# Converting the weights of a feed-forward early: bit work on float64 weights during attention, a float32 copy in DRAM, and a first chunk that only splits

## The chip, the cores and the metric

The kernel runs on one core of a Trainium2 chip. The time is that of the device in microseconds for one execution; of several runs the median counts. TensorE (PE) multiplies matrices, DVE (VectorE), ACT (ScalarE) and POOL (GpSimd) work on elements, SP (SyncE) issues the DMAs.

## The reference

```python
scores = scale * q @ k.T - log(S)            # 8 batches, 12 heads, S = 448, head_dim 64
x = heads_side_by_side(sigmoid(scores) @ v)  # (8, 448, 768)
u = x + real(fft(fft(x, axis=1), axis=2))    # mixing
un = (u - mean(u)) / sqrt(var(u) + 1e-6)     # over the last axis
out = u + maximum(un @ w_ch1, 0) @ w_ch2     # 768 -> 3072 -> 768
```

q, k and v are float32. The two weight matrices are float64.

## The kernel before

**Attention and mixing.** Two heads make a group g; 48 groups (G), six for a batch. A group has four steps t (192 in all): `scores(t)` makes the scores of 112 keys for two heads in PSUM (`sc`, two buffers), ACT makes the sigmoid `a` (L126, five buffers), and two steps later `values(t)` multiplies by v into the one bank `av`. After the fourth step DVE copies `av` into `xT` (L151). Because the f32 matmuls are rounded, q and k are split in two parts: POOL rounds (`cast`, L107: `qh`, `kh`), DVE subtracts (`rest`, L112: `ql`, `kl`). A batch's Fourier transform is done by matrices (`mix_units`): POOL and a little DVE fold xT (`fold`, L165 to L171), TensorE multiplies (`psd`, `pss`) and transposes (`psx`), DVE adds `u` (L223), SP stores `u` in DRAM (`u_dram`). These units are spread over the steps of the next batch.

**Order.** The code is written out in pairs of steps: first what the pair before left over (`flush`: sp_next, act_next, dve_next), then scores, values, mixing units, and then whatever a table `extra` has for these steps; `at(t, fn)` puts something there. `pin` keeps each engine's instructions in the order in which the code names them, so an engine that waits for one instruction holds all behind it. All DMAs go through SP's queue.

**Weights.** A matrix has 24 slices (NFC) of 128 x 768 float64, so 48 slices of 768 KB. Each is read twice. First, during attention: `weight_load` brings it into one of three buffers `wr` (pairs of int32), and `weight_max` on DVE takes the largest absolute high word (L254). At step TP = 170 `weight_scales` makes one scale per matrix. Then, from step TP on, `prep_w` reads each slice again (L356) and converts it: ACT takes the absolute high word (L365, n = 1), DVE clamps and shifts (L367, L369, n = 2), DVE joins low word and sign (L373, L375, n = 3), and in n = 4 ACT scales (L381) and rounds to float16 (`w1h` or `w2h`, L382) and POOL subtracts (`w1l` or `w2l`, L383). The result of n = 1 to 4 stands in one of three buffers `wt`. `prep_step` spreads these parts over slots, two for each f of the first chunk.

**Feed-forward.** There are 7 chunks c of 512 tokens. `norm` normalises a chunk: it loads `un` from `u_dram`, DVE takes statistics and an inverse root in many small operations on `mv` (L297 to L319), DVE scales (L322), ACT rounds to float16 in a buffer `hl` that has the tag `wt` too (L328), DVE subtracts (L332), SP transposes into `uh`, `ul` (L334). For each f of 24, `up_proj` is 18 matmuls into `psh` (L516), ACT and DVE make `hh` and `hl` (L523, L524), and `down_proj` of the f before is 24 matmuls into `po` (L535). `finish` adds `u` and stores. Between attention and the first chunk the rest of the mixing runs (`mix_rest`), with slots in between.

Of the kernel before, what the change touches and what calls it, by code (L numbers as in the profile page):

```python
# [36 lines left out]
LNT = 2  # L37
UNIT_US = 0.57
MIX_UP = 8
MIX_STEP = 7  # L40
# [10 lines left out]
def spectral_attention_ffn(tc, q, k, v, w1, w2, cd, cs, ident_in, out):  # L51
# [8 lines left out]
    with ExitStack() as top:  # L60
        cpool = top.enter_context(tc.tile_pool(name="cpool", bufs=1))
        dram = top.enter_context(tc.tile_pool(name="dram", bufs=1, space=DRAM))
        u_dram = dram.tile([NT, DM], F32, name="u_dram")
        ident = cpool.tile([128, 128], F32, name="ident")
# [13 lines left out]
        if True:  # L78
# [178 lines left out]

            def weight_scales():
# [4 lines left out]

                wi = ws.bitcast(I32)
                nc.vector.tensor_scalar(
                    out=wi[:, 0:2], in0=wi[:, 0:2], scalar1=20, scalar2=0x7FF,
                    op0=ALU.logical_shift_right, op1=ALU.bitwise_and)
                nc.vector.tensor_scalar(
                    out=wi[:, 0:2], in0=wi[:, 0:2], scalar1=1023 - 60, scalar2=1023 + 60, op0=ALU.max, op1=ALU.min)
                nc.vector.tensor_scalar(  # L270
                    out=wi[:, 0:2], in0=wi[:, 0:2], scalar1=-896, scalar2=1 << 23, op0=ALU.add, op1=ALU.mult)
# [80 lines left out]
            def prep_w(i, f, n):  # L352

                if n == 0:
                    prep[i, f] = r = wpre.tile([128, DM, 2], I32, tag="wr", name="wr", bufs=3)
                    nc.sync.dma_start(  # L356
                        r.rearrange("p n w -> p (n w)"), (w1, w2)[i][:, f * 2 * DM:(f + 1) * 2 * DM])
                    return
                if n == 1:
                    prep[i, f] = prep[i, f], wpre.tile([128, DM], F32, tag="wt", name="wt", bufs=3)  # L360
                r, t = prep[i, f]
                ti = t.bitcast(I32)
                lo, hi = r[:, :, 0], r[:, :, 1]
                if n == 1:
                    nc.scalar.activation(t, hi.bitcast(F32), AF.Abs)  # L365
                elif n == 2:
                    nc.vector.tensor_scalar(  # L367
                        out=t, in0=t, scalar1=HI_MIN, scalar2=HI_MAX, op0=ALU.max, op1=ALU.min)
                    nc.vector.tensor_scalar(  # L369
                        out=ti, in0=ti, scalar1=3, scalar2=0x3FFFFFF8,  # L370
                        op0=ALU.logical_shift_left, op1=ALU.bitwise_and)
                elif n == 3:
                    nc.vector.scalar_tensor_tensor(  # L373
                        out=ti, in0=lo, scalar=29, in1=ti, op0=ALU.logical_shift_right, op1=ALU.bitwise_or)
                    nc.vector.scalar_tensor_tensor(  # L375
                        out=ti, in0=hi, scalar=-0x40000000, in1=ti, op0=ALU.bitwise_and, op1=ALU.bitwise_or)
                elif n == 4:
                    h, l = (x[f] for x in ((w1h, w1l), (w2h, w2l))[i])
                    if i == 0:
# [303 lines left out]
```

## Time and profile before

| what | value |
|---|---|
| median of 3 runs | 1817.26 us (1816.38 to 1821.08) |
| profiled execution | 1819.07 us, its span 1817.3 us |
| TensorE busy | 1748.8 us (96%) |
| DVE busy | 677.1 us (37%) |
| ACT busy | 434.2 us (24%) |
| POOL busy | 278.5 us (15%) |
| DMA | 166.56 MB, mean 92 GB/s |
| granted clock of TensorE, mean | 0.992 |

The span goes from the first to the last instruction. The shares are means over stages that differ: attention runs to about 447 us, the rest of the mixing to 470, the first chunk to 690, and six more chunks follow. A granted clock of 1.00 is 2.4 GHz, the upper of two levels; the lower is 1.2 GHz.

### The profile page before, as it was taken

The numbers are of one execution on the slowest core, as the hardware profiler recorded it, in microseconds if no ns is written. First come the engines' busy times: TensorE is split into PE (matmuls) and PEld (weight loads), VectorE is DVE, ScalarE is ACT, GpSimd is POOL, SyncE is SP. The second block draws the span as 40 slices with busy tenths as digits, with TensorE's granted clock in tenths as the row PEclk, the third lists the DMA queues.
The fourth block names the chain that finished last, engine by engine and source line by source line (L and its number), as shares of the span: only waits on it lengthen the run. The fifth ranks groups of instructions, "written<-read, shape, count | busy, mean of one in ns | idle before, by whom it ended". The sixth has DMA issues, their size and how long they took to land.

```text
span 1817.3 us, 22712 instructions
## 1 busy us (share of the span) xinstructions
PE 1748.8 (96%) x9616; PEld 927.0 (51%) x9616; DVE 677.1 (37%) x1143; ACT 434.2 (24%) x581; POOL 278.5 (15%) x268
## 2 busy tenths in 40 slices
PE   8999999988888889999999999999999999999998
PEld 4555555545444445555555555555555555555554
DVE  3445576656999985200320033002400200010001
ACT  4434444435556641000100001000100000000000
POOL 4534444335344430000000000000000000000000
PEclk9999999999999999999999999999999999999999
DMA  7666677654555535000400040004000400010000
GB/s 233 217 210 207 234 222 223 206 188 118 173 170 174 170 127 152 4 1 1 136 4 1 1 122 18 1 1 122 18 1 1 105 18 1 1 43 11 1 1 35
DMA packets 92280, 166.56 MB, mean 92 GB/s; under 512 B 49697, under 2 KB 62738, under 8 KB 92050
## 3 DMA queue, kind: packets, MB, share of 16 engines
q1 hardware_dynamic: 92178, 165.11, 29.3%
q8 instruction: 75, 1.23, 0.3%
q14 instruction: 27, 0.22, 0.0%
HBM read 132.05 MB, written 22.02 MB: 85 GB/s over the span
## 4 chain that ended last, share of the span: by engine, by line
PE 59%; DVE 13%; DMA 2%; issue 1%; ACT 0%; DVEq 0%; ACTq 0%; SPq 0%
PE po L535 30%; PE psh L516 30%; DVE wt L375 5%; DVE wt L373 2%; DVE wt L369 1%; DVE wt L367 1%; DMA un<-u_dram 1%; DVE hl L524 1%; DMA y_out<-ur 1%; DVE ur L556 0%; DVE stt L297 0%; DVE hl L332 0%; DVE u L223 0%; DVE un L322 0%; DVE mv L317 0%
## 5 line engine op out<-in xcount | busy, mean ns | idle before, releaser
L535 PE MATMUL po<-w2h,hl 128*128 128x512 f16 (+1 forms) x1344 | 439.9, 327 | 26.8 <-DVE hl L524 26.8
L535 PE MATMUL po<-w2h,hh 128*128 128x512 f16 (+1 forms) x1344 | 439.9, 327 | 5.0 <-ACT hh L523 4.3
L535 PE MATMUL po<-w2l,hh 128*128 128x512 f16 (+1 forms) x1344 | 439.6, 327 | 0.0
L524 DVE SCALAR_TENSOR_TENSOR hl<-psh,hh 128x512 f16<-128x512 f32 x168 | 115.6, 688 | 833.1 <-ACT hh L523 833.1
L516 PE MATMUL psh<-uh,w1h 128*128 128x512 f16 x1008 | 382.0, 379 | 0.0
L516 PE MATMUL psh<-ul,w1h 128*128 128x512 f16 x1008 | 382.0, 379 | 0.0
L516 PE MATMUL psh<-uh,w1l 128*128 128x512 f16 x1008 | 382.0, 379 | 0.0
L535 PEld LDWEIGHTS <-hh 128*128 128x128 f16 x2688 | 262.5, 98 | 182.6 <-ACT hh L523 12.7
L523 ACT ACTIVATE hh<-psh 128x512 f16<-128x512 f32 x168 | 99.8, 594 | 942.1 <-PE psh L516 942.1
L516 PEld LDWEIGHTS <-w1h 128*128 128x128 f16 x2016 | 197.3, 98 | 236.7
L126 ACT ACTIVATE a<-sc 112x900 f32<-112x900 f32 x192 | 166.7, 918 | 161.1 <-PE sc L122 161.1
L535 PEld LDWEIGHTS <-hl 128*128 128x128 f16 x1344 | 131.9, 98 | 123.1 <-DVE hl L524 38.1
L142 PE MATMUL av<-a,vr 112*64 112x450 f32 x768 | 169.6, 563 | 3.5 <-DVE xT L151 3.5
L516 PEld LDWEIGHTS <-w1l 128*128 128x128 f16 x1008 | 98.6, 98 | 118.9
L375 DVE SCALAR_TENSOR_TENSOR wt<-wr,wt 128x768 int32<-128x768 int32 x48 | 100.4, 2092 | 1.7
L122 PE MATMUL sc<-qh,kh 64*112 64x450 f32 x384 | 81.7, 421 | 10.8 <-ACT a L126 5.2
L142 PEld LDWEIGHTS av<-a,vr 112*64 112x64 f32 x768 | 47.4, 138 | 82.0 <-issue 67.3
L151 DVE TENSOR_SCALAR xT<-av 128x450 f32<-128x450 f32 x48 | 30.1, 626 | 135.0 <-PE av L142 134.9
L184 PEld LDWEIGHTS psd<-cd_sb,xp 128*113 128x113 f32 x384 | 61.1, 178 | 32.8 <-issue 29.7
L184 PE MATMUL psd<-cd_sb,xp 128*113 128x193 f32 x384 | 74.7, 338 | 1.8 <-DVE xp L171 1.8
L122 PE MATMUL sc<-qh,kl 64*112 64x450 f32 x384 | 73.6, 379 | 1.7 <-DVE kl L112 1.7
L122 PE MATMUL sc<-ql,kh 64*112 64x450 f32 x384 | 73.3, 377 | 0.0
(61 smaller groups left out, 1115.8 us busy)
## 6 DMA issues: line engine op xcount, KB each, us to landing
wr<-w_in SPq DMA_DIRECT2D x96, 768.0 KB, 4.7
qr<-q_in SPq DMA_DIRECT2D x48, 225.0 KB, 3.5
kr<-k_in SPq DMA_DIRECT2D x48, 224.0 KB, 3.1
vr<-v_in SPq DMA_DIRECT2D x24, 448.0 KB, 4.0
un<-u_dram SPq DMA_DIRECT2D x14, 768.0 KB, 5.6
ur<-u_dram SPq DMA_DIRECT2D x14, 768.0 KB, 5.6
y_out<-ur SPq DMA_DIRECT2D x12, 768.0 KB, 7.4
u_dram<-u SPq DMA_DIRECT2D x24, 336.0 KB, 3.8
```

The costliest lines, as they stand in the source:

```text
L122: nc.tensor.matmul(ps[:CP, j, :SQ], split[g, 1, kn][h, c * CP:(c + 1) * CP], split[g, 0, qn][h], start=(n == 0), stop=(n == 2))
L126: nc.scalar.activation(a, ps[:CP, :, :SQ], AF.Sigmoid, bias=-math.log(S), scale=1.0 / math.sqrt(D))
L142: nc.tensor.matmul(ps[j * D:(j + 1) * D, :SQ], vr[:, c, h * D:(h + 1) * D], a[:, j], start=(c == 0), stop=(c == 3))
L151: nc.vector.tensor_scalar(out=xT[:, p].rearrange("d r k -> d (r k)"), in0=ps[:, :SQ], scalar1=1.0, scalar2=None, op0=ALU.mult)
L184: nc.tensor.matmul(ps[:HM, par * 193:par * 193 + 193], xp[:, kp ^ c, c, par, p], cd_sb[:, c, par, p], start=(p == 0), stop=(p == 2))
L367: nc.vector.tensor_scalar(out=t, in0=t, scalar1=HI_MIN, scalar2=HI_MAX, op0=ALU.max, op1=ALU.min)
L373: nc.vector.scalar_tensor_tensor(out=ti, in0=lo, scalar=29, in1=ti, op0=ALU.logical_shift_right, op1=ALU.bitwise_or)
L375: nc.vector.scalar_tensor_tensor(out=ti, in0=hi, scalar=-0x40000000, in1=ti, op0=ALU.bitwise_and, op1=ALU.bitwise_or)
L516: nc.tensor.matmul(hs[c, f], l[f][:, m], r[:, m], start=(m == n == 0), stop=(m == NCC - 1 and n == 2))
L523: nc.scalar.activation(hh, ps, AF.Relu)
L524: nc.vector.scalar_tensor_tensor(out=hl, in0=ps, scalar=0.0, in1=hh, op0=ALU.max, op1=ALU.subtract)
L535: nc.tensor.matmul(po[n][:, at:at + hi - lo], l[:, cols], r[f][:, lo:hi], start=(f == 0 and m == 0 and at == 0), stop=(f == NFC - 1 and m ...
```

## The change

During attention each slice is now loaded once and converted there (`weight_step`): load (k = 0, five steps ahead), absolute value on ACT (k = 1), clamp on POOL (k = 2), shift and low word on DVE (k = 3), sign and maximum on DVE (k = 4), and a store of the float32 slice into a DRAM tensor `w_dram` (k = 5). The first chunk's slots load 384 KB of float32, two slots ahead (`AHEAD`); ACT scales and rounds in one operation, DVE makes the low part. Chunk 1's norm moves from attention into chunk 0. The first slots after attention come every four instead of seven steps of the mixing rest.

```diff
+AHEAD = 2
-MIX_STEP = 7
+MIX_STEP = 4
...
+        w_dram = dram.tile([2 * NFC, 128, DM], F32, name="w_dram")
...
-            def weight_max(n):
-                i, f = divmod(n, NFC)
-                nc.vector.tensor_reduce(
-                    out=wmax[:, i, f:f + 1], in_=wtile.pop(n)[:, :, 1].bitcast(F32), op=ALU.max, axis=AX.X,
-                    apply_absolute_value=True)
+            def weight_step(n, k):
+
+                i, f = divmod(n, NFC)
+                if k == 0:
+                    wtile[n] = r = wpre.tile([128, DM, 2], I32, tag="wr", name="wr", bufs=3)
+                    nc.sync.dma_start(
+                        r.rearrange("p n w -> p (n w)"), (w1, w2)[i][:, f * 2 * DM:(f + 1) * 2 * DM])
+                    return
+                if k == 1:
+                    wtile[n] = wtile[n], wpre.tile([128, DM], F32, tag="wt", name="wt", bufs=3)
+                r, t = wtile[n]
+                ti = t.bitcast(I32)
+                lo, hi = r[:, :, 0], r[:, :, 1]
+                if k == 1:
+                    nc.scalar.activation(t, hi.bitcast(F32), AF.Abs)
+                elif k == 2:
+                    nc.gpsimd.tensor_scalar(
+                        out=t, in0=t, scalar1=HI_MIN, scalar2=HI_MAX, op0=ALU.max, op1=ALU.min)
+                elif k == 3:
+                    nc.vector.tensor_scalar(
+                        out=ti, in0=ti, scalar1=3, scalar2=0x3FFFFFF8,
+                        op0=ALU.logical_shift_left, op1=ALU.bitwise_and)
+                    nc.vector.scalar_tensor_tensor(
+                        out=ti, in0=lo, scalar=29, in1=ti, op0=ALU.logical_shift_right, op1=ALU.bitwise_or)
+                elif k == 4:
+                    nc.vector.scalar_tensor_tensor(
+                        out=ti, in0=hi, scalar=-0x40000000, in1=ti, op0=ALU.bitwise_and, op1=ALU.bitwise_or)
+                    nc.vector.tensor_reduce(
+                        out=wmax[:, i, f:f + 1], in_=t, op=ALU.max, axis=AX.X, apply_absolute_value=True)
+                else:
+                    nc.sync.dma_start(w_dram[i * NFC + f], t)
+                    del wtile[n]
...
+            def prep_step(k):
+
+                if k < len(order):
+                    prep[k] = t = wpre.tile([128, DM], F32, tag="wt", name="wt", bufs=3)
+                    i, f = order[k]
+                    nc.sync.dma_start(t, w_dram[i * NFC + f])
+                k -= AHEAD
+                if k in prep:
...
+                    sc = wsc[:, i:i + 1]
+                    nc.scalar.activation(h, t, AF.Copy, scale=sc)
+                    nc.vector.scalar_tensor_tensor(
+                        out=l, in0=t, scalar=sc, in1=h, op0=ALU.mult, op1=ALU.subtract)
...
+            for n in range(2 * NFC):
+                t = 14 + n * (TP - 20) // (2 * NFC)
+                for j, d in enumerate((-5, 0, 1, 2, 3, 5)):
+                    at(t + d, lambda n=n, j=j: weight_step(n, j))
             at(TP, weight_scales)
...
+            for j in range(NPRE + AHEAD):
+                at(TP + (2 if j < AHEAD else 4 * (j - AHEAD) + 6), lambda j=j: prep_step(j))
+            for g in range(2):
+                for n, fn in norm_plan(0, g, fx):
+                    at(24 * (4 + g) + LNT + n, fn)
...
-                n = step % MIX_STEP
-                if n < 4 and slot < NPRE + 2 * NW2:
-                    prep_step(slot, n)
-                    slot += n == 3
+                if step % MIX_STEP == 0 and slot < NPRE + 2 * NW2:
+                    prep_step(slot + AHEAD)
+                    slot += 1
...
-                    if 2 <= c + 1 < NCK:
+                    if c + 1 < NCK:
```

Left out of the diff: the removal of `weight_load`, `prep_w` and the old `prep_step`, and `weight_scales`, which now takes the power of two of the scale by one mask instead of shift and multiply.

DVE's order in attention, in a group of four steps of a batch whose mixing is at its `u` additions. Before (one `xT` to the next):

```order
L151 TENSOR_SCALAR xT<-av 128x450
L254 TENSOR_REDUCE wmax<-wr 128x1
L112 TENSOR_TENSOR ql<-qr,qh 128x450
L112 TENSOR_TENSOR kl<-kr,kh 128x448
L204 TENSOR_TENSOR sm<-pss,Q 112x385
L204 TENSOR_TENSOR df<-pss,Q 112x385
L223 TENSOR_TENSOR u<-psx,df 113x384
L223 TENSOR_TENSOR u<-psx,sm 113x384 x2
L151 TENSOR_SCALAR xT<-av 128x450
```

The same group after the change, with one slice's operations (L266 to L274):

```order
L153 TENSOR_SCALAR xT<-av 128x450
L114 TENSOR_TENSOR ql<-qr,qh 128x450
L114 TENSOR_TENSOR kl<-kr,kh 128x448
L266 TENSOR_SCALAR wt<-wt 128x768
L269 SCALAR_TENSOR_TENSOR wt<-wr,wt 128x768
L206 TENSOR_TENSOR sm<-pss,Q 112x385
L206 TENSOR_TENSOR df<-pss,Q 112x385
L272 SCALAR_TENSOR_TENSOR wt<-wr,wt 128x768
L274 TENSOR_REDUCE wmax<-wt 128x1
L225 TENSOR_TENSOR u<-psx,df 113x384
L225 TENSOR_TENSOR u<-psx,sm 113x384 x2
L153 TENSOR_SCALAR xT<-av 128x450
```

One maximum has become a shift, two joins and a maximum, ahead of the additions `u` and the next `xT`.

SP's order after the change where the first half of chunk 0's norm ends, with buffer numbers: wt_2479 is a slice, hl_2538 and hl_2582 are the norm's, and hl_2582 is the third buffer of the tag `wt` after wt_2479 (between them hl_2538 and wt_2570), so it takes that slice's place.

```order
L252 DMA wr_2533<-w2_in 128x1536
L353 DMA_TRANSPOSE uh_2536<-hl_2538 128x6x128
L353 DMA_TRANSPOSE ul_2537<-hl_2538 128x6x128
L98 DMA kr_2577<-k_in 128x448
L99 DMA qr_2576<-q_in 128x450
L277 DMA w_dram_61<-wt_2479 128x768
L252 DMA wr_2621<-w2_in 128x1536
L353 DMA_TRANSPOSE uh_2536<-hl_2582 128x6x128
```

The store that frees wt_2479 stands behind two transposes and two loads; before there were no stores of slices and no `wt` tiles in these steps. ACT's order at the same place:

```order
L128 ACTIVATE a_2557<-sc_2550 112x900
L261 ACTIVATE wt_2570<-wr_2431 128x768
L347 ACTIVATE hl_2582<-un_2277 128x768
L128 ACTIVATE a_2591<-sc_2584 112x900
L128 ACTIVATE a_2600<-sc_2593 112x900
```

Two sigmoids stand behind hl_2582; before, the absolute value was not there.

DVE's order in the first chunk, from one `hl` to the next, before:

```order
L524 SCALAR_TENSOR_TENSOR hl<-psh,hh 128x512
L367 TENSOR_SCALAR wt<-wt 128x768
L369 TENSOR_SCALAR wt<-wt 128x768
L373 SCALAR_TENSOR_TENSOR wt<-wr,wt 128x768
L375 SCALAR_TENSOR_TENSOR wt<-wr,wt 128x768
L367 TENSOR_SCALAR wt<-wt 128x768
L369 TENSOR_SCALAR wt<-wt 128x768
L373 SCALAR_TENSOR_TENSOR wt<-wr,wt 128x768
L375 SCALAR_TENSOR_TENSOR wt<-wr,wt 128x768
L524 SCALAR_TENSOR_TENSOR hl<-psh,hh 128x512
```

After:

```order
L511 SCALAR_TENSOR_TENSOR hl<-psh,hh 128x512
L386 SCALAR_TENSOR_TENSOR w2l_4733<-wt,wsc,w2h_4712 128x768
L386 SCALAR_TENSOR_TENSOR w1l_4694<-wt,wsc,w1h_4687 128x768
L511 SCALAR_TENSOR_TENSOR hl<-psh,hh 128x512
L386 SCALAR_TENSOR_TENSOR w2l_4734<-wt,wsc,w2h_4713 128x768
L386 SCALAR_TENSOR_TENSOR w1l_4695<-wt,wsc,w1h_4688 128x768
L511 SCALAR_TENSOR_TENSOR hl<-psh,hh 128x512
```

Eight operations between two `hl` have become two.

## Rows read from the trace of the kernel before

**Rows 1.** Windows by stage: TensorE, weight loads, DVE, ACT, POOL busy; clock, DMA share, GB/s.

```profile
0.00:100.00 100.00, 93.25 (x565) 47.93 (x566) 45.41 (x61) 47.88 (x57) 46.04 (x59) 1.00 0.71 222
100.00:200.00 100.00, 95.16 (x578) 53.47 (x578) 46.48 (x70) 43.06 (x55) 41.52 (x49) 0.98 0.63 207
200.00:300.00 100.00, 94.78 (x574) 52.34 (x571) 70.25 (x130) 43.10 (x55) 40.68 (x48) 0.98 0.68 222
300.00:400.00 100.00, 90.71 (x536) 49.82 (x535) 58.91 (x109) 43.37 (x55) 38.40 (x44) 0.97 0.68 216
470.00:690.00 220.00, 190.28 (x969) 93.05 (x969) 205.64 (x239) 122.03 (x152) 82.51 (x43) 0.98 0.51 163
690.00:1818.00 1128.00, 1121.07 (x6053) 591.86 (x6051) 198.56 (x444) 99.60 (x162) 0.00 (x0) 1.00 0.11 31
```

**Rows 2.** Waits of TensorE: who for whom, us, times, longest.

```profile
PE po L535 <- DVE hl L524: 26.8, 22, 3.1
PE psx L216 <- DVE u L223: 13.8, 7, 2.7
```

**Rows 3.** Timeline of DVE, two starts of hl in the first chunk.

```profile
492.55 0.68 DVE L524 SCALAR_TENSOR_TENSOR hl<-psh,hh 128x512 f16<-128x512 f32 x1
501.90 0.68 DVE L524 SCALAR_TENSOR_TENSOR hl<-psh,hh 128x512 f16<-128x512 f32 x1
```

**Rows 4.** Timeline of TensorE at 470 us, then the chain of waits near the end.

```profile
470.07 0.38 PE L535 MATMUL po<-w2h,hh 128*128 128x512 f16 x1 [0.72 <-DVE u L223]
...
1781.38 3.90 PE po L535 x24
1785.28 3.88 PE psh L516 x18
1804.73 5.00 PE po L535 x30
```

**Rows 5.** Groups of instructions by form, whole execution.

```profile
L375 DVE SCALAR_TENSOR_TENSOR wt<-wr,wt 128x768 int32<-128x768 int32 x48 | 100.4, 2092 | 1.7
L254 DVE TENSOR_REDUCE wmax<-wr 128x1 f32<-128x768 f32 x48 | 45.3, 944 | 0.0
L365 ACT ACTIVATE wt<-wr 128x768 f32<-128x768 f32 x48 | 43.4, 904 | 0.7 <-DMA wr<-w_in 0.7
L107 POOL TENSOR_SCALAR kh<-kr 128x448 fp32r<-128x448 f32 x48 | 30.4, 632 | 6.1 <-DMA kr<-k_in 6.1
L369 DVE TENSOR_SCALAR wt<-wt 128x768 int32<-128x768 int32 x48 | 27.4, 570 | 1.6
L332 DVE TENSOR_TENSOR hl<-un,hl 128x768 f16<-128x768 f32 x28 | 26.3, 956 | 20.6 <-ACT hl L328 20.5
```

**Rows 6.** Timeline of DVE, then of POOL.

```profile
420.20 0.96 DVE L375 SCALAR_TENSOR_TENSOR wt<-wr,wt 128x768 int32<-128x768 int32 x1
480.93 2.28 DVE L375 SCALAR_TENSOR_TENSOR wt<-wr,wt 128x768 int32<-128x768 int32 x1
...
480.76 1.64 POOL L383 TENSOR_TENSOR w2l<-wt,w2h 128x768 f16<-128x768 f32 x1 [2.74 <-ACT w2h L382]
```

**Rows 7.** Instructions of tile wr: count, ns min/median/max, first and last start.

```profile
L254 DVE TENSOR_REDUCE wmax<-wr x48: 898/944/992, 33.2 to 372.1; 128x1 f32<-128x768 f32 x48
```

**Rows 8.** Groups of DVE from 100 to 200 us, then its timeline.

```profile
L112 DVE TENSOR_TENSOR kl<-kr,kh 128x448 fp32r<-128x448 f32 x11 | 9.9, 898 | 0.0
L112 DVE TENSOR_TENSOR ql<-qr,qh 128x450 fp32r<-128x450 f32 x11 | 8.2, 745 | 0.0
L151 DVE TENSOR_SCALAR xT<-av 128x450 f32<-128x450 f32 x10 | 6.3, 627 | 42.7 <-PE av L142 42.7
...
122.58 0.61 DVE L112 TENSOR_TENSOR kl<-kr,kh 128x448 fp32r<-128x448 f32 x1
```

**Rows 9.** Timeline of ACT and TensorE at 422 us.

```profile
421.78 0.84 ACT L328 ACTIVATE hl<-un 128x768 f16<-128x768 f32 x1 [7.12 <-DVE un L322]
423.97 0.72 PE L122 MATMUL sc<-qh,kh 64*112 64x450 f32 x2 [4.58 <-ACT a L126]
```

More of the change, by code (lines that the diff above doesn't have):

```diff
@@ L262, in weight_scales @@
                 nc.gpsimd.partition_all_reduce(ws[:, 0:2], wm, 128, bass_isa.ReduceOp.absmax)
+                nc.vector.tensor_scalar(
+                    out=ws[:, 0:2], in0=ws[:, 0:2], scalar1=2.0 ** -60, scalar2=2.0 ** 60, op0=ALU.max, op1=ALU.min)
                 wi = ws.bitcast(I32)
                 nc.vector.tensor_scalar(
[L266 to L271, printed above, removed]
+                    out=wi[:, 0:2], in0=wi[:, 0:2], scalar1=0x7F800000, scalar2=None, op0=ALU.bitwise_and)
                 nc.vector.reciprocal(ws[:, 2:4], ws[:, 0:2])
@@ L350, in spectral_attention_ffn @@
                 order += [(1, f)] + [(0, f + NPRE)] * (f + NPRE < NFC)
[L352 to L377, printed above, removed]
+            def prep_step(k):
[5 more added lines that the diff above has]
+                if k in prep:
+                    i, f = order[k]
+                    t = prep.pop(k)
                     h, l = (x[f] for x in ((w1h, w1l), (w2h, w2l))[i])
@@ L380, in prep_w @@
                         h, l = (x.rearrange("p c f -> p (c f)") for x in (h, l))
-                    nc.scalar.activation(t, t, AF.Copy, scale=wsc[:, i:i + 1])
-                    nc.scalar.activation(h, t, AF.Copy)
-                    nc.gpsimd.tensor_tensor(out=l, in0=t, in1=h, op=ALU.subtract)
-            def prep_step(k, n):
-                for d, m in (((2, 0), (-1, 4)), ((1, 1),), ((0, 2),), ((0, 3),))[n]:
-                    if k + d < len(order) and (k + d, m) not in prepped:
-                        prepped.add((k + d, m))
-                        prep_w(*order[k + d], m)
+                    sc = wsc[:, i:i + 1]
+                    nc.scalar.activation(h, t, AF.Copy, scale=sc)
+                    nc.vector.scalar_tensor_tensor(
+                        out=l, in0=t, scalar=sc, in1=h, op0=ALU.mult, op1=ALU.subtract)
             act_next, dve_next, sp_next, units = [], [], [], []
@@ L437, in spectral_attention_ffn @@
             TP = max(TQ - 4 * NPRE - 10, 1)
-            when_w = {}
-            for n in range(2 * NFC):
-                when_w.setdefault(14 + n * (TP - 14) // (2 * NFC), []).append(n)
             extra = {}
@@ L489, in spectral_attention_ffn @@
                         fn()
-                    for n in when_w.get(i - 1, ()):
-                        weight_load(n + 2)
-                    for n in when_w.get(i, ()):
-                        weight_max(n)
                 pin()
@@ L598, in spectral_attention_ffn @@
                     for n in range(2):
-                        if c == 0 and slot <= len(order):
-                            for step in range(4):
-                                prep_step(slot, step)
+                        if c == 0 and slot < len(order):
+                            prep_step(slot + AHEAD)
                             slot += 1
```

17 lines of the change are left out of this document (removed).

## The prediction

> **What bounds the kernel now.** The windows come first [rows 1]. From 690 us to its last matmul's end at 1809.73 TensorE is never idle (1121.07 us busy by modelled ends), so nothing there can gain. Between 470 and 690 us, the feed-forward's first chunk, TensorE is busy 190.28 of 220 us and DVE 205.64: DVE is the full engine there. Before 400 us TensorE is 91 to 95% busy, DVE 45 to 70%, POOL 38 to 46%. The waits of TensorE say the same [rows 2]: the longest sum is for `hl`, which stands in DVE's queue behind two weight slices. The timeline gives that loop's period [rows 3]: `hl` starts at 492.55 and at 501.90, so 9.35 us for one f. Later chunks show what TensorE alone needs [rows 4]: 3.90 us for a down projection and 3.88 for an up projection, 7.783 us for the pair (three pairs from 1781.38 to 1804.73).
>
> **What the first chunk gives back.** The first down projection starts at 470.07 and the last ends at 1804.73 + 5.00 = 1809.73 [rows 4]: 1339.66 us. At TensorE's own pace it would be 166 pairs x 7.783 + 2 x 3.90 = 1299.8 us (two up projections are done before). The 39.9 us between them are DVE's: 22 f x 1.57 = 34.5 us, the rest the start of the chunk and a clock that fell after waits.
> After the change a slice costs DVE one scalar_tensor_tensor over 768 elements, f32 in and f16 out. The nearest row is the f16 `hl` of the norm at 956 ns [rows 5]; two of them and one 0.68 us `hl` are 2.6 us of the 7.8 us that TensorE needs, where a slice's four operations filled (9.35 - 0.68) / 2 = 4.3 us. ACT loses the absolute value and one of two copies for each slice, POOL its whole part, and the DMA reads half the bytes. Chunk 1's norm moves into this chunk, as it runs in every later one, where TensorE never waits. I keep 1.5 us for the start: **-38 us**. Bounds: 30 (if a wait at the start and the extra norm stay) to 40.
>
> **What attention pays on DVE.** Before, a slice cost DVE one maximum, 944 ns. It keeps that (over contiguous data now) and gets a shift-and (570 ns), and two scalar_tensor_tensor, each 957 ns when nothing is in the way [rows 5, 6]: 0.57 + 2 x 0.957 = 2.48 us more. The 48 maxima ran from 33.2 to 372.1 us [rows 7], 7.1 us apart or 339 / 150 = 2.26 us a step, and the new plan has nearly the same pace, so 14 slices in 100 us: +35 us of DVE in 100.
> On top come waits for POOL. The row to see [rows 6]: the same scalar_tensor_tensor took 0.96 us at 420.20 and 2.28 us at 480.93, where it began while POOL's subtraction (480.76, 1.64 us) ran, and ended 0.8 us after it. That it waits out POOL's instruction is what the Trainium skill says in "SBUF — State Buffer", Who interferes with whom: a DVE operation with two SBUF inputs and a GpSimd operation that reads SBUF exclude each other for a whole instruction. By that rule each new operation with two inputs is exposed, where the free 0.96 us alone would make the sum some 19 us better. How much of it counts is read from attention itself, where `kl` and `ql` average 898 and 745 ns [rows 8] against 610 when free (122.58 in [rows 8]), so 0.2 us an operation with POOL 42% busy. The clamp goes to POOL; there is no such operation of 768 elements in the trace; its bounds are the cast of 448 elements, 0.63 us [rows 5], and the subtraction, 1.64 us; I take the cast by length, 768/448 x 0.632 = 1.08. 14 clamps make POOL 57% busy, so I price the wait at 0.27 us: 3 x 14 x 0.27 = 11 us, and 2 for `ql` and `kl`, in 100. Bounds of the wait: 0 and 1.3 us an operation.
> So DVE's load in 100 us [rows 1]: 100 to 200, 46.5 + 35 + 13 = **94**; 200 to 300, where chunk 0's norm stands, 70.3 + 48 = **118**; 300 to 400, less about 10 for half of chunk 1's norm (the two halves of chunk 0's are most of the 24 us by which 200 to 300 exceeds 100 to 200) and with slices up to 372, 58.9 - 10 + 0.72 x 48 = **83**; 0 to 100, 45.4 + 0.67 x 48 = **78**. DVE was idle 42.7 us in 100 to 200 waiting for `av` alone [rows 8]: that idle time is the cover, and it is used up.
>
> **What that does to TensorE.** `xT` empties the only `av` bank and stands in DVE's queue; TensorE needs it one step later, and `psx` waits for `u` already in each batch (13.8 us in all, [rows 2]). In the order of the change, the four steps with the first `u` get 2.5 us more of DVE; the next four get two shift-ands and three scalar_tensor_tensor for one maximum, 3.2 us more, some 10.0 in all with each operation at 0.5 to 1 us. Nine of these are exposed, 2.4 us: 12.4 us against the 4 x 2.26 = 9.0 of the steps and the 2 that TensorE waits for `u` there already. About +2 us in each of the four to five batches that have slices and no norm: **+10**, and **+6** for uneven steps and clock. In 200 to 320 us the overload of 18 in 100 us ends on TensorE: **+18**. A second wait falls in the same place: `hl` of the norm and the weight tiles share three buffers `wt`; the second `hl` on ACT takes the buffer of a slice whose store is queued on SP behind two transposes, and the sigmoids stand behind that `hl`. The trace has one such case [rows 9]: ACT idle 7.12 us before `hl`, TensorE 4.58 us (such stalls also cost clock: 0.97 and 0.98 are granted here, [rows 1]). Twice that and its clock, some 12 us, lies within the 18, since DVE catches up meanwhile. That very stall, from chunk 1's norm, goes away: **-5**. Attention: 10 + 6 + 18 - 5 = **+29**; bounds 10 (no waits for POOL: DVE 82 and 105 in 100) and 55 (0.5 us an operation).
>
> Free, with what covers it: ACT's 48 absolute values (904 ns, [rows 5]) against an ACT 43% busy; stores of 48 x 384 KB, 14 x 0.393 MB in 100 us or 55 GB/s more on DMA engines 0.63 to 0.71 busy at 207 to 222 GB/s [rows 1], about 0.87; if that cover went, a late `wr` would hold ACT's queue and with it the sigmoids. SP gets 48 stores that wait for DVE; behind them stand `kr`, `qr` loads with five steps (11 us) to spare. The scales lose one operation on two elements.
>
> **Sum.** 1817.3 - 38 + 29 = 1808; of the waits in the mixing rest (0.72 us stands before the first down projection, [rows 4]) 1 us goes too: **1807 us** of span. The profiled execution took 1819.07 us, 1.8 above the median of 1817.26, so on the median's scale the change is -10: 1807.
>
> **Rivals.**
> 1. Attention hides more: the waits for POOL seldom meet, or DVE's lateness is bridged by the five `a` buffers. For it: TensorE's largest wait there, for `u`, is 13.8 us in eight batches. Against it: 118 in 100 cannot be hidden. Attention +12: 1790 us.
> 2. Slower, by DVE and POOL excluding each other. In a batch (24 steps, 55 us) POOL now works 0.415 x 55 = 23 us and then 7.7 x 1.08 = 8 more, and the exposed DVE work is 12 x 0.61 + 7.7 x 2.48 = 26 us: together more than the batch itself. If the two queues alternate, as in the first chunk, where the mean of 2092 ns says that some 41 of 48 took the long time, each operation waits 0.5 to 0.6 us and DVE is over 100 in 100 throughout. It decides from a mean wait of about 0.4 us. Five batches x 5, norm 25, clock 8, less 5: +53; 1832 us. The Trainium skill's rule (the section above) speaks for this rival.
> 3. No change within 0.3% (5.5 us, about what a measurement here can tell): attention takes back 33 to 44 us, the same mechanism at 0.33 us an operation: 1817 us.
> 4. The first chunk is held by something else: `w_dram` loads late behind transposes on SP. Against it: a slice is used four f, 31 us, after its slot. 1820 us.
>
> **Chances.** Forecast (1799 to 1812) 0.38; rival 1 (1782 to 1799) 0.24; rival 3 0.16; rival 2 0.18; rival 4 0.04. Faster: 0.38 + 0.24 less a little for the forecast's upper edge, 0.60; within 0.3%: 0.18; slower: rival 2 and half of 4, 0.22. Range: from rival 1's price, 1788, to rival 2's, 1832; the likeliest's own is 1799 to 1812.
>
> **What would show it.** First chunk: `hl` 7.8 us apart, TensorE over 98% busy, DVE under 50%. Attention: DVE over 90% busy in 100 to 300 us, scalar_tensor_tensor means of 1.2 us, TensorE's idle time ended by `u`, `xT` and ACT, its clock under 1.00, and the mixing rest beginning 25 to 35 us later than before. It is wrong if scalar_tensor_tensor in attention means over 1.4 us or 0.97, if TensorE waits in the norm stretches for under 8 or over 35 us, or if the first chunk still waits for DVE.

## The result, and the profile after

The changed kernel takes 1833.84 us (median of 4 runs, 1831.8 to 1836.21), the kernel before 1816.82 beside it: a ratio of 1.0089 with a 95% interval of [1.0067, 1.0112]. It is slower by 0.9%, where a gain to 1807 was forecast in a range of 1788 to 1832. The execution shown here took 1836.21 us, its span 1834.3.

Where the time went shows when the windows are cut at the start of the first down projection. First the stage ahead of it in the kernel before (columns as in [rows 1]):

```profile
0.00:470.07 470.07, 437.46 (x2596) 242.11 (x2597) 272.91 (x463) 212.59 (x268) 196.03 (x225) 0.98 0.64 204
```

After the change, the same stage, then the rest, then four stretches inside the stage:

```profile
0.00:528.58 528.58, 462.40 (x2597) 253.57 (x2597) 406.19 (x532) 243.22 (x303) 360.83 (x268) 0.92 0.65 206
528.58:1840.00 1311.42, 1300.48 (x7021) 686.64 (x7019) 281.09 (x611) 151.20 (x230) 0.00 (x0) 1.00 0.15 44
...
0.00:100.00 100.00, 87.01 (x483) 43.86 (x484) 68.40 (x74) 50.85 (x60) 67.59 (x55) 0.91 0.74 226
100.00:200.00 100.00, 84.60 (x484) 46.09 (x483) 86.07 (x103) 44.80 (x57) 85.59 (x59) 0.91 0.68 216
200.00:300.00 100.00, 88.46 (x503) 47.47 (x502) 85.83 (x122) 49.58 (x63) 70.96 (x49) 0.93 0.74 239
300.00:400.00 100.00, 78.77 (x419) 43.35 (x417) 87.30 (x122) 38.70 (x49) 73.42 (x53) 0.86 0.71 229
```

The stage has become 528.58 - 470.07 = 58.5 us longer. TensorE ran the same 2597 matmuls; they kept it busy 462.40 instead of 437.46 us, and it was idle 66.2 instead of 32.6: 24.9 us went to slower matmuls (clock 0.92 for 0.98), 33.6 to idle time.

The rest of the kernel, timeline and chain of waits of TensorE after the change:

```profile
528.58 0.38 PE L522 MATMUL po<-w2h,hh 128*128 128x512 f16 x1
...
1821.83 5.00 PE po L522 x30
```

From there to the end of this chain on TensorE it is 1826.83 - 528.58 = 1298.25 us, 41.4 less than the 1339.66 of [rows 4]. 58.5 - 41.4 = 17.1, and the spans differ by 17.0: these two numbers are the whole result. (1826.83 is where the chain of waits leaves TensorE; its last matmul ends at 1829.63. Before, these were 1809.73 and 1812.53, so the difference is the same.)

What TensorE waits for now, and the groups of the slice's operations (POOL's clamp, DVE's two joins, shift and maximum):

```profile
PE psx L218 <- DVE u L225: 29.7, 8, 7.7
PE psx L218 <- DVE df L206: 10.6, 5, 3.7
PE av L144 <- DVE xT L153: 8.5, 5, 3.2
```

```profile
L263 POOL TENSOR_SCALAR wt<-wt 128x768 f32<-128x768 f32 x48 | 142.6, 2973 | 59.4 <-ACT wt L261 57.2
L269 DVE SCALAR_TENSOR_TENSOR wt<-wr,wt 128x768 int32<-128x768 int32 x48 | 64.0, 1333 | 1.7
L272 DVE SCALAR_TENSOR_TENSOR wt<-wr,wt 128x768 int32<-128x768 int32 x48 | 55.5, 1156 | 0.5
L266 DVE TENSOR_SCALAR wt<-wt 128x768 int32<-128x768 int32 x48 | 48.4, 1008 | 11.5 <-POOL wt L263 11.4
L274 DVE TENSOR_REDUCE wmax<-wt 128x1 f32<-128x768 f32 x48 | 45.8, 953 | 1.6
```

The wait for `u` was 13.8 us before [rows 2]; with the waits for `df` it is now 40.3. The longest one can be followed on DVE (timeline of DVE, then of POOL and of TensorE, after the change):

```profile
177.31 0.63 DVE L153 TENSOR_SCALAR xT<-av 128x450 f32<-128x450 f32 x1 [0.52 <-PE av L144]
178.02 1.41 DVE L266 TENSOR_SCALAR wt<-wt 128x768 int32<-128x768 int32 x1
179.47 1.20 DVE L269 SCALAR_TENSOR_TENSOR wt<-wr,wt 128x768 int32<-128x768 int32 x1
180.59 0.97 DVE L114 TENSOR_TENSOR ql<-qr,qh 128x450 fp32r<-128x450 f32 x1
181.48 1.48 DVE L114 TENSOR_TENSOR kl<-kr,kh 128x448 fp32r<-128x448 f32 x1
182.89 1.73 DVE L272 SCALAR_TENSOR_TENSOR wt<-wr,wt 128x768 int32<-128x768 int32 x1
184.66 0.95 DVE L274 TENSOR_REDUCE wmax<-wt 128x1 f32<-128x768 f32 x1
185.53 1.01 DVE L225 TENSOR_TENSOR u<-psx,df 113x384 f32<-113x384 f32 x2
...
182.44 1.36 POOL L167 TENSOR_TENSOR eo<-xT 128x450 f32<-128x450 f32 x1
183.89 3.36 POOL L263 TENSOR_SCALAR wt<-wt 128x768 f32<-128x768 f32 x1
...
186.13 0.90 PE L218 MATMUL psx<-ident,xT 128*112 128x128 f32 x3 [7.69 <-DVE u L225]
186.96 0.71 PE L124 MATMUL sc<-qh,kh 64*112 64x450 f32 x2
191.59 0.45 PE L124 MATMUL sc<-qh,kh 64*112 64x450 f32 x2
```

DVE has no pause here. Between `xT` and the first `u` stand a slice's four operations and `ql`, `kl`: 7.5 us, where they would take 0.57 + 0.96 + 0.61 + 0.61 + 0.96 + 0.95 = 4.7 if nothing held them (free durations of [rows 5, 6, 8]). TensorE stands still for 7.69 us, and the first pair of score matmuls afterwards takes 0.71 us, the one at 191.59 again 0.45. Windows of 10 us show it as a clock that falls after the pause:

```profile
170.00:180.00 10.00, 7.58 (x50) 4.11 (x46) 9.29 (x12) 4.79 (x6) 9.84 (x8) 1.00 0.70 232
180.00:190.00 10.00, 3.87 (x19) 2.48 (x21) 9.80 (x12) 1.34 (x2) 8.78 (x6) 0.66 0.58 194
190.00:200.00 10.00, 10.00 (x65) 5.70 (x59) 7.50 (x10) 5.57 (x8) 7.44 (x7) 1.00 0.43 129
```

### The profile page after: what moved, and what is told of

The parts are those of the page before. It is cut to its first block, busy times and chain, and to the rows that moved or that the text cites. A ratio compares the mean times of both kernels' runs of the same rounds, so it can differ in the third digit from the quotient of the medians.

```text
span 1834.3 us, 22884 instructions
## 1 busy us (share of the span) xinstructions
PE 1762.9 (96%) x9616; PEld 940.2 (51%) x9616; DVE 687.3 (37%) x1142; ACT 394.4 (22%) x533; POOL 360.8 (20%) x268
## 4 chain that ended last, share of the span: by engine, by line
PE 80%; DVE 7%; POOL 4%; issue 4%; DMA 3%; ACT 0%; SPq 0%; DVEq 0%; POOLq 0%; ACTq 0%
PE po L522 35%; PE psh L503 35%; PE av L144 3%; PE sc L124 3%; PE psd L186 2%; POOL wt L263 2%; DMA w_dram<-wt 1%; DVE wt L272 1%; DMA qr<-q_in 1%; DVE wt L269 1%; DVE wt L266 1%; DVE kl L114 1%; PE psx L218 1%; POOL eo L167 1%; DVE ql L114 1%
## 5 line engine op out<-in xcount | busy, mean ns | idle before, releaser
L144 PE MATMUL av<-a,vr 112*64 112x450 f32 x768 | 178.1, 588 | 8.5 <-DVE xT L153 8.5
L263 POOL TENSOR_SCALAR wt<-wt 128x768 f32<-128x768 f32 x48 | 142.6, 2973 | 59.4 <-ACT wt L261 57.2
L186 PEld LDWEIGHTS psd<-cd_sb,xp 128*113 128x113 f32 x384 | 64.6, 187 | 35.2 <-issue 31.7
L186 PE MATMUL psd<-cd_sb,xp 128*113 128x193 f32 x384 | 78.6, 351 | 2.8 <-DVE xp L173 2.8
L218 PE MATMUL psx<-ident,xT 128*113 128x128 f32 (+1 forms) x192 | 33.3, 307 | 40.3 <-DVE u L225 29.7
```

The costliest lines, as they stand in the source:

```text
L144: nc.tensor.matmul(ps[j * D:(j + 1) * D, :SQ], vr[:, c, h * D:(h + 1) * D], a[:, j], start=(c == 0), stop=(c == 3))
L186: nc.tensor.matmul(ps[:HM, par * 193:par * 193 + 193], xp[:, kp ^ c, c, par, p], cd_sb[:, c, par, p], start=(p == 0), stop=(p == 2))
L218: nc.tensor.transpose(ps[:HM - kp, i * 128:(i + 1) * 128], xT[:, hf * 3 + i, r, kp:HS:2], ident)
L263: nc.gpsimd.tensor_scalar(out=t, in0=t, scalar1=HI_MIN, scalar2=HI_MAX, op0=ALU.max, op1=ALU.min)
```

## The experiments

The expectations were written for two theories: that POOL's long clamp costs the time in attention (P), and that DVE's queue does, where the slice's operations, held by POOL's, stand ahead of `u`, `df` and `xT` (D). A third (L) came with the kernel with reductions: that the waits of DVE and POOL for each other carry the loss. Two numbers tell a run: the start of the first down projection (before 470.07, after 528.58), which is attention's price, and the time from there to the end. Each is read from one execution, and the times of one kernel's executions lie 2 to 12 us apart, so a difference of 2 or 3 us between two starts says little. All ratios are to the kernel before.

**The clamp: on DVE, left out, replaced.** Three kernels change `k == 2` of `weight_step` alone (in this order):

```diff
-                    nc.gpsimd.tensor_scalar(
+                    nc.vector.tensor_scalar(
```

```diff
-                    nc.gpsimd.tensor_scalar(
-                        out=t, in0=t, scalar1=HI_MIN, scalar2=HI_MAX, op0=ALU.max, op1=ALU.min)
+                    pass
```

```diff
-                        out=t, in0=t, scalar1=HI_MIN, scalar2=HI_MAX, op0=ALU.max, op1=ALU.min)
+                        out=t, in0=t, scalar1=1.0, scalar2=0.0, op0=ALU.mult, op1=ALU.add)
```

> The changed kernel with the clamp moved from POOL to DVE, nothing else. Theory P (the clamp on POOL, 2.97 us instead of the 1.08 that was priced, makes POOL late and with it casts, folds and DVE): POOL falls below 45% busy in 100 to 200 us, TensorE's idle time before 400 us falls from 64 us to below 40, and the time is 1795 to 1810 us although DVE gets 48 x 0.56 us more. Rival D (DVE's own added load is what costs): DVE is over 95% busy and the time is 1834 us or more.

> The clamp is left out of the computation, on every engine. Theory P: the time falls to 1788 to 1800 us, the price of the clamp on POOL is then some 40 us. Rival D: DVE keeps its shift, two joins and the waits, so the time stays above 1825 us.

> POOL does a multiplication by one and an addition of zero in place of maximum and minimum, same tile and size, so the clamp is left out of the computation. If the length of the clamp comes from its operations, it takes about 1.1 us as the cast did by length, and theory P then gives 1798 to 1812 us, the first forecast. If it comes from 768 elements in place, it stays near 2.8 us and the time at 1834 us. Rival D: 1828 us or more in either case.

On DVE: 1830.0 us, ratio 1.0061 [1.0046, 1.0076], first down projection at 526.65. Left out: 1812.31, 0.9959 [0.9944, 0.9974], 508.38. Replaced by a multiplication and addition on POOL: 1823.53, 1.0026 [1.0013, 1.0039], 516.77, with this group:

```profile
L263 POOL TENSOR_SCALAR wt<-wt 128x768 f32<-128x768 f32 x48 | 49.8, 1038 | 110.2 <-ACT wt L261 109.9
```

P falls as the whole cause: with POOL relieved of the clamp (234.47 us busy in the stage for 360.83) only 2 us come back (4 by the median times), since DVE then carries it. D was missed too, in all three: it had 1834 us or more, over 1825, and 1828 or more. The clamp counts wherever it stands, some 20 us; its length over the priced 1.08 us counts 11.8 (528.58 - 516.77). With that price met, attention would still have paid 46.7 us.

**DVE's bit work.** Two kernels change `k == 3` and `k == 4`. The first leaves out shift and joins, the second puts reductions of about the same length, with one input, in their place:

```diff
-                    nc.vector.tensor_scalar(
-                        out=ti, in0=ti, scalar1=3, scalar2=0x3FFFFFF8,
-                        op0=ALU.logical_shift_left, op1=ALU.bitwise_and)
-                    nc.vector.scalar_tensor_tensor(
-                        out=ti, in0=lo, scalar=29, in1=ti, op0=ALU.logical_shift_right, op1=ALU.bitwise_or)
+                    nc.vector.tensor_reduce(out=junk[:, 0:1], in_=t, op=ALU.max, axis=AX.X)
+                    nc.vector.tensor_reduce(out=junk[:, 1:2], in_=t, op=ALU.max, axis=AX.X)
...
-                    nc.vector.scalar_tensor_tensor(
-                        out=ti, in0=hi, scalar=-0x40000000, in1=ti, op0=ALU.bitwise_and, op1=ALU.bitwise_or)
+                    nc.vector.tensor_reduce(out=junk[:, 2:3], in_=t[:, 0:464], op=ALU.max, axis=AX.X)
```

> The clamp stays on POOL; DVE's shift and two joins are left out of the computation, DVE keeps the maximum. Theory P: POOL stays at 75% or more in 100 to 200 us and the time at 1818 us or more. Rival D: DVE is back at 50 to 60% and the time falls to 1785 to 1798 us. Both loads needed together: between 1798 and 1818 us here and in the kernel without the clamp.

> DVE's shift and two joins (0.57 + 2 x 0.957 us) are left out of the computation and replaced by reductions of the same tile that take as long when nothing is in the way (2 x 0.953 and one of 464 elements, some 0.58 us) and have one SBUF input, like the maximum that was never lengthened. The clamp stays on POOL. Rival L (the waits of DVE and POOL for each other, some 1 us a slice by the means of 1008, 1333 and 1156 ns, carry the loss): the time falls to 1805 to 1815 us. Rival D (DVE's own added load carries it, whatever its form): 1822 to 1834 us. Without any of that load the kernel took 1786.

Without bit work: 1786.28 us, 0.9811 [0.9791, 0.9831]; with reductions: 1805.14, 0.9924 [0.9906, 0.9941]. The windows up to the first down projection, of the one and of the other:

```profile
0.00:479.13 479.13, 443.61 (x2596) 243.34 (x2597) 249.51 (x388) 241.64 (x303) 323.27 (x268) 0.97 0.70 228
```

```profile
0.00:497.18 497.18, 448.86 (x2596) 245.36 (x2597) 348.26 (x532) 242.30 (x303) 321.43 (x268) 0.96 0.68 219
```

Groups of DVE in the kernel with reductions:

```profile
L267 DVE TENSOR_REDUCE junk<-wt 128x1 f32<-128x768 f32 x48 | 45.4, 945 | 11.2 <-POOL wt L264 10.7
L268 DVE TENSOR_REDUCE junk<-wt 128x1 f32<-128x768 f32 x48 | 45.2, 942 | 0.0
L270 DVE TENSOR_REDUCE junk<-wt 128x1 f32<-128x464 f32 x48 | 30.0, 625 | 0.0
```

The second is as theory L expected (1805 to 1815 us). The two divide the 58.5 us. All that remains without bit work, the stores, ACT, POOL's clamp and the moved norm among it, costs 479.13 - 470.07 = 9.1. Work of the bare length, 0.945 + 0.942 + 0.625 = 2.51 us a slice, costs 18.0 more. That shift and joins hold and are held by POOL's operations costs another 528.58 - 497.18 = 31.4, over half. The reductions are not held: their means are those of a maximum alone. They differ in one thing more: they neither read `wr` nor write `wt`, so buffers and stores come free earlier. That was not tested apart; in the changed kernel ACT waits in this stage 2.6 us for loads of `wr` and 3.2 us for stores of `wt`, which leaves little room for it.

The clamp is not what holds most. In the changed kernel's trace shift and joins take 49.7 us more than free; 37.5 of it falls to operations that overlap only other instructions of POOL, the casts and folds, and 6.9 to those that overlap the clamp alone. With the clamp on DVE, clamp, shift and joins still take 35 us more than free, which fits the small gain of that kernel.

The Trainium skill says as much in "SBUF — State Buffer", Who interferes with whom: a reduction never contends with GpSimd, while operations with two SBUF inputs do (against one of GpSimd that reads SBUF), and `tensor_scalar`, the shift, can when its operands meet certain conditions. The trace agrees: 942 to 953 ns for reductions, 1333 and 1156 for the joins, 1008 for the shift.

**Half of the slices early.** Only `w1` is converted during attention, `w2` in the first chunk (its old four operations on DVE; `cut` does scaling, rounding and low part). The second of these kernels takes only steps without `u`, `df` and norm for it, the third is the first with the clamp on DVE:

```diff
+                    cut(j - 1, True)
...
-                t = 14 + n * (TP - 20) // (2 * NFC)
+                t = 14 + (2 * f + i) * (TP - 20) // (2 * NFC)
```

```diff
+            calm = [t for t in range(14, TP - 6)
+                    if (t < 29 or (t - 29) % 24 < 13) and not 98 <= t < 113 and not 122 <= t < 137]
...
-                t = 14 + (2 * f + i) * (TP - 20) // (2 * NFC)
+                t = calm[f * len(calm) // NFC] if i == 0 else 17 + f * (TP - 23) // NFC
```

> Only the 24 slices of the first matrix are converted during attention and stored; those of the second are only loaded for their maximum there and are converted in the first chunk as before the change. Slices of both alternate. DVE in the first chunk then has one conversion (4.3 us), one split (1.0) and hl (0.7) for each f, 6.0 us of the 7.8 that TensorE needs, so rival D expects nearly the whole 40 us there and under half of the 58 us in attention: 1790 to 1805 us, faster than both kernels. If the loss in attention comes from something that every version with stores has (SP's queue, the wt buffers), attention stays 40 us or more longer: 1815 us or more.

> As the kernel that converts half of the slices early, but these 24 stand only in steps that have neither the last mixing stages (df, u) nor chunk 0's norm; the second matrix's maxima are spread evenly, and loads go three steps ahead instead of five. If the loss comes from where conversions stand in DVE's queue (ahead of df and u, for which TensorE's psx waits), it is 5 to 12 us below the kernel with the even spread. If only the sum of DVE's work counts, it is the same within 3 us, or slower, since the calm steps get fuller.

> As the kernel that converts half of the slices early with the even spread, with the clamp of these on DVE instead of POOL (0.57 us for 2.9). Where all 48 were converted early this was worth 4 us; with half of them 2 us or nothing: 1788 to 1803 us.

The first: 1836.18 us, 1.0089 [1.0068, 1.0111], first down projection at 505.22. In calm steps: 1828.4, 1.0049 [1.003, 1.0068], 493.98. With the clamp on DVE: 1826.33, 1.0037 [1.0022, 1.0052], 492.01. Attention pays 35.2, 23.9 and 21.9. All three missed their expected times. D had expected under 29 for the first; keeping away from `u` and the norms saves 11.2; and the clamp on DVE, worth 2 us or nothing by its expectation and 1.9 in the start with all 48 slices, saves 13.2 here. So POOL's clamp does cost where DVE has room to take it over.

But the first chunk did not become TensorE's: all three need 1324 to 1326 us from their first down projection to the end. The first of the three shows why: TensorE's waits after the first down projection, the window from there to the end, and timelines of ACT and then TensorE.

```profile
PE po L569 <- ACT hh L557: 18.7, 5, 5.7
...
505.22:1840.00 1334.78, 1309.02 (x7021) 687.84 (x7019) 338.07 (x674) 184.78 (x272) 35.83 (x22) 0.99 0.16 49
...
567.05 0.84 ACT L360 ACTIVATE hl<-un 128x768 f16<-128x768 f32 x1 [8.85 <-DMA ul<-hl]
593.39 0.93 ACT L395 ACTIVATE wt<-wt,wsc 128x768 f32<-128x768 f32 x1 [4.12 <-DVE wt L421]
596.72 0.58 ACT L557 ACTIVATE hh<-psh 128x512 f16<-128x512 f32 x1
601.42 0.93 ACT L395 ACTIVATE wt<-wt,wsc 128x768 f32<-128x768 f32 x1 [4.12 <-DVE wt L421]
...
573.58 0.39 PE L569 MATMUL po<-w2h,hh 128*128 128x512 f16 x1 [4.70 <-ACT hh L557]
```

`hh` stands behind four weight operations, the first of which waits for DVE, and DVE's next operations stand behind the `hl` made from that `hh`: a ring of 8.03 us a turn. That is only 0.25 us above TensorE's 7.78 and not the main loss. TensorE waits 18.7 us in five stalls, and its matmuls are busy 1309.02 - 1300.48 = 8.5 us longer than in the changed kernel; together these are the 27.2 us that this kernel needs more (1325.4 for 1298.25). Four of the five stalls follow right after an `hl` of chunk 1's norm on ACT: there ACT stands 6 to 9 us, for DVE's `un` or for the transposes of the `hl` before, and `hh` stands behind it. The other two kernels have the same five stalls, 16.9 and 16.4 us. In the kernel before this norm stood in attention. No run took it out of the chunk again.

**`hh` and `hl` first.** The calm kernel, with the clamp on DVE and the evacuation ahead of the slot's weight work:

```diff
+                        if n == 0 and (c or f):
+                            evac(c, f)
                         if c == 0 and slot <= len(order):
                             prep_step(slot + AHEAD)
                             slot += 1
-                        if n == 0 and (c or f):
-                            evac(c, f)
```

> Only w1 is converted during attention (24 slices, none in steps with u, df or a norm), w2 in the first chunk; the clamp is on DVE; and in the first chunk hh and hl of an f are queued ahead of that slot's weight work instead of behind it. Theory D (DVE's in-order queue in attention, mostly by two-input operations meeting POOL's): attention pays +14 to +22 us over before, and with hh and hl ahead of the weight work the first chunk goes from 1325 back to 1298 to 1305 us; 1788 to 1800 us in all. Rival (the first chunk with half of the bit work is held by DVE and POOL excluding each other, not by the order of the queue): the chunk stays at 1320 to 1326 us and the time at 1815 to 1825.

1809.34 us, 0.9937 [0.9916, 0.9957]: faster than before. Attention pays 20.7 (first down projection at 490.77), and the rest takes 1310.7 us. D was right on attention (+14 to +22); in the first chunk the order brought 13 us of the 20 to 27 expected, and the time lies above the expected 1800. Two waits for `hh` are left, 8.2 us in all, both behind an `hl` of chunk 1's norm.

**Nothing early.** Three kernels go back to the kernel before and change its first chunk alone: POOL clamps one slot ahead, and DVE makes the low part with the scale in it, in place of ACT's scaling and POOL's subtraction. The second adds the order of `evac` above, the third queues the low part behind the next slice's joins:

```diff
                     nc.scalar.activation(t, hi.bitcast(F32), AF.Abs)
+                    nc.gpsimd.tensor_scalar(
                         out=t, in0=t, scalar1=HI_MIN, scalar2=HI_MAX, op0=ALU.max, op1=ALU.min)
...
+                    nc.scalar.activation(h, t, AF.Copy, scale=sc)
+                    nc.vector.scalar_tensor_tensor(
+                        out=l, in0=t, scalar=sc, in1=h, op0=ALU.mult, op1=ALU.subtract)
```

```diff
-                for d, m in (((2, 0), (-1, 4)), ((1, 1),), ((0, 2),), ((0, 3),))[n]:
+                for d, m in (((2, 0), (-1, 4)), ((1, 1),), ((0, 2),), ((0, 3), (-1, 5)))[n]:
```

> The kernel before, with its conversion still in the first chunk, and only two things changed there: the clamp goes to POOL, and the low part is made by one scalar_tensor_tensor on DVE with the scale in it, so that ACT's in-place scaling and POOL's subtraction go away. Nothing is converted in attention. Theory D: attention is that of before, the first down projection starts at 470 +- 2 us; DVE's work for one f is 2 x (0.57 + 0.96 + 0.96 + 0.96) + 0.68 = 7.6 us if the clamp lets the joins through, just under TensorE's 7.78, so the first chunk falls from 1340 to 1300 to 1312 us: 1778 to 1790 us. Rival (POOL's clamp of 2.8 us, twice in each f, holds DVE's two-input operations for its length as the subtraction of 1.64 us did): 2 us of waiting for each of two slices, hl 10 to 12 us apart, 1840 us or more.

> As the kernel with the late POOL clamp, and hh and hl of an f queued ahead of the slots' weight work in the first chunk. Theory D: the same as that kernel or up to 8 us less, as hl no longer stands behind a slice's operations: 1775 to 1788 us. Rival (POOL's clamp holds the joins): as slow as that kernel, since DVE's work for one f is then over 7.8 us in either order.

> As the kernel with the late POOL clamp and hh and hl ahead of the weight work, with one change of order on DVE: the low part of the slice before is queued behind a slot's shift and joins and not ahead of them. In the two late kernels a join takes 0.96 us even while POOL clamps, so the clamp does not hold it; their 5.10 us a slice read as a ring: ACT's rounding 0.94, DVE's low part 1.02, shift 1.18 (0.57 where POOL is idle) and two joins 1.92, and the next rounding waits for the second join. Theory ring: with the low part behind the joins the rounding is done meanwhile, DVE is the full engine at 2 x (1.18 + 1.92 + 1.02) + 0.68 = 8.9 us for one f, hl 8.8 to 9.0 us apart, the first chunk 1325 to 1332 us from its first down projection to the end and the time 1802 to 1812. Rival (POOL's clamp and the ACT behind it set the 5.1 us a slice, whatever the order): hl stays 10.2 us apart and the time at 1826 to 1832.

The first two took 1831.25 us, 1.0055 [1.0033, 1.0077], and 1827.74, 1.0045 [1.003, 1.006]. Neither theory held: the joins took 0.96 us, so the clamp does not hold them, and yet `hl` came 10.2 us apart. The timeline of the first, DVE and then ACT:

```profile
571.02 1.02 DVE L383 SCALAR_TENSOR_TENSOR w1l<-wt,wsc,w1h 128x768 f16<-128x768 f32 x1 [0.40 <-ACT w1h L382]
571.95 1.18 DVE L369 TENSOR_SCALAR wt<-wt 128x768 int32<-128x768 int32 x1
573.16 0.96 DVE L373 SCALAR_TENSOR_TENSOR wt<-wr,wt 128x768 int32<-128x768 int32 x1
574.16 0.96 DVE L375 SCALAR_TENSOR_TENSOR wt<-wr,wt 128x768 int32<-128x768 int32 x1
576.12 1.02 DVE L383 SCALAR_TENSOR_TENSOR w2l<-wt,wsc,w2h 128x768 f16<-128x768 f32 x1 [1.00 <-ACT w2h L382]
...
570.05 0.94 ACT L382 ACTIVATE w1h<-wt,wsc 128x768 f16<-128x768 f32 x1 [2.89 <-DVE wt L375]
575.15 0.93 ACT L382 ACTIVATE w2h<-wt,wsc 128x768 f16<-128x768 f32 x1 [3.36 <-DVE wt L375]
```

ACT rounds only after the second join, and DVE's next shift stands behind the low part that waits for that rounding: 575.15 - 570.05 = 5.10 us a slice, two for each f. The third kernel opens this ring: 1799.38 us, 0.9895 [0.9863, 0.9928], the fastest kernel that does the whole computation. Its `hl` come 8.46 us apart, from the first down projection (473.17) to the end it takes 1316.8, all three below what the ring theory expected (1802 to 1812, 8.8 to 9.0, 1325 to 1332). Attention converts nothing; its start of the first down projection is 3.1 us later than before, 1.65 of them one wait for `u`. Timeline of DVE and of POOL in it:

```profile
568.28 0.55 DVE L369 TENSOR_SCALAR wt<-wt 128x768 int32<-128x768 int32 x1
568.86 1.56 DVE L373 SCALAR_TENSOR_TENSOR wt<-wr,wt 128x768 int32<-128x768 int32 x1
570.45 0.96 DVE L375 SCALAR_TENSOR_TENSOR wt<-wr,wt 128x768 int32<-128x768 int32 x1
571.33 1.01 DVE L387 SCALAR_TENSOR_TENSOR w2l<-wt,wsc,w2h 128x768 f16<-128x768 f32 x1
...
568.78 2.77 POOL L366 TENSOR_SCALAR wt<-wt 128x768 f32<-128x768 f32 x1 [0.83 <-ACT wt L365]
```

**A fourth buffer.** The changed kernel with `bufs=4` in place of 3 for the tag `wt`:

```diff
-                    wtile[n] = wtile[n], wpre.tile([128, DM], F32, tag="wt", name="wt", bufs=3)
+                    wtile[n] = wtile[n], wpre.tile([128, DM], F32, tag="wt", name="wt", bufs=4)
```

> The changed kernel with four instead of three buffers of the tag wt, and nothing else. In the changed kernel's trace the chain of waits passes four times between 60 and 420 us through a store of a slice into DRAM (5.3 to 7.4 us each, 6.8% of these 360 us), behind which ACT's absolute value of a later slice takes the buffer. Theory D (DVE's queue: the slice's operations stand ahead of u, df and xT, stretched by POOL): the fourth buffer lets absolute value and clamp start earlier but changes nothing in DVE's work, so the first down projection starts at 524 to 530 us and the time is 1828 to 1836. Rival (the ring of three buffers makes the bursts: slices come late and then together): the first down projection starts 10 us or more earlier, at 500 to 518 us, and the time is 1805 to 1824.

1832.36 us, 1.0076 [1.0059, 1.0093], first down projection at 528.16: the ring of `wt` buffers is not the cause in attention.

## Why the prediction was wrong

**First chunk: right.** -41.4 measured, -38 forecast, bounds 30 to 40. It is over the upper bound because the prediction took 1809.73 for the end of the last matmul, which is 1812.53: what stood above TensorE's own pace of 1299.8 was 42.7 us and not 39.9. `hl` comes 7.8 us apart, TensorE is busy 1300.48 us of what is left, and DVE 110.44 of the 222 us from 528 to 750, just under 50%.

**What attention pays on DVE: near in its sum, in part for other reasons.** The joins take 1333 and 1156 ns (1.24 on average, 1.2 forecast), 0.58 us of waiting a slice where 2 x 0.27 = 0.54 was priced. The shift, which has one input, is held too: 1008 instead of 570 ns, 0.44 us. The prediction's reason named only operations with two inputs, but its sum counted three a slice, 0.81 us, for 1.01 measured. The clamp takes 2.97 us where 1.08 was taken from a cast by length, above the upper bound of 1.64, and that counts 11.8 us (the run with a clamp of 1.04 us). The forecast DVE loads of 94 and 118 in 100 did not show as such: it was 86 and 86. DVE and TensorE wait for each other in turn here, and the stage became longer before DVE was full.

**What that does to TensorE: this is the step that failed.** +29 was forecast, bounds 10 to 55, and 58.5 measured. Of the 29.5 us between them, 18.9 are the term for clock and 10.6 the waits:
- +6 for uneven steps and clock. TensorE's busy time for the same matmuls grew by 24.9 us. This is the largest error. After the stall at 186 us the clock was 0.66 in that window, between its two levels of 2.4 and 1.2 GHz; over the stage 33.6 us of more idle time came with 24.9 of slower work.
- +10 for `u` (2 us in each of four or five batches) and +18 for the norm stretch. All idle time grew by 33.6. The waits for `u` and `df` together grew by 26.5, and not only in the norm stretch, where the load was forecast largest: the window from 100 to 200 us, which holds no norm, has the longest wait and loses 10.6 us of busy time (95.16 to 84.60). By the prediction's own numbers a batch without norm gave 12.4 - 9.0 - 2 = 1.4 us and not 2. The cover was taken as DVE's idle time over a batch; what counted at the longest stall is the queue between one `xT` and the next `u`, 7.5 us in the rows above.
- -5 for chunk 1's norm. Its stall of 4.58 us [rows 9] is gone, but behind chunk 0's norm TensorE now waits for `a` twice, 3.9 us in all. That stall was also no case of the buffer that the prediction feared: ACT waited there for DVE's `un`.

**The rivals.** Rival 2 gave 1832 and the sign, by the mechanism that the kernel with reductions confirms: POOL and DVE holding each other are worth 31.4 us. That its number came so near is partly luck. The mean wait of the three new operations was 1.01 / 3 = 0.34 us, where it asked for 0.5 to 0.6 and rival 3 had no change at 0.33; DVE was not over 100 in 100; and the clock took 24.9 us for its 8. Rivals 1 and 3 are out by the same rows. Of rival 4 there is 14.1 us of waiting of ACT for late slices of `w1` (7 times) and 4.4 for those of `w2` (3 times); TensorE waits 0.6 us in all after the first down projection.

**Open.** How the 24.9 us of clock and 33.6 of idle time divide over the single causes was not separated: every kernel that shortened the waits regained clock too (busy 443.61 us without bit work, 448.86 with reductions). The move of chunk 1's norm and the new `MIX_STEP` were not run apart; they lie in the 9.1 us that remain without bit work. Moving only some `w1` slices on top of the fastest kernel was not run.

## What to carry to other kernels

Idle time of an engine with an ordered queue is no cover by its sum: count what stands in the queue between one handover to TensorE and the next, at the durations that they have while the other engines work, and add the clock that each stall of some microseconds costs afterwards. Before work is moved out of a full stage, look whether that stage is full or only waits in a ring: here two changes of order, the clamp moved to POOL, and ACT's scaling and POOL's subtraction made one operation on DVE gained 1.05% together (without the last change of order they lost 0.5%), where moving all the work lost 0.9%. A replaced operation is priced by its own kind: on POOL a clamp by max and min took 2.9 times as long as a multiplication and addition over the same tile.

## What was not expected of the hardware

POOL's `tensor_scalar` of 128 x 768 float32 takes 2.97 us (mean) with max and min, and 1.04 with mult and add.

This clamp, as the profile's rough spans of POOL show it, holds one operation of DVE for some 0.6 us in its first part, and none to its end. In the last timeline above it runs from 568.78 to 571.55; the join that starts 0.08 us later takes 1.56 instead of 0.96, the next one, all inside it, 0.96, and the low part 1.01. If the shift is the operation at its start, it takes 1.18 instead of 0.55 (571.95 above). In these two kernels (the last of the three and the first) the shifts, joins, low parts, `ql` and `kl` that ran inside a clamp were held if they began within 0.82 us of its start, 42 in each kernel and at most one to a clamp; those that began 1.27 us after it or later, 40 and 43, took their free time. That DVE's two-input operations are held for POOL's whole instruction, as the Trainium skill has it in "SBUF — State Buffer", Who interferes with whom, and as POOL's subtraction does in [rows 6], is not borne out by this clamp: 0.6 us of 2.77.
